# First batch's dilated values read from the load's own buffer, one tail-value load per batch, and a new table of scheduling biases

## The chip, the cores and the metric

One core of a Trainium2 chip runs the whole program. The metric is the device time of one execution in microseconds (us). The engines named here are PE (TensorE, matrix multiplication and transposes; PEld is its weight load), DVE (VectorE), ACT (ScalarE), POOL (GpSimd) and SP (SyncE, which here only issues DMAs). A DMA moves data between DRAM and the core's memory; SP and POOL each have a queue of them. "L901" is line 901 of the kernel before; behind L408 the changed file is one to eleven lines longer.

## What is computed

Two stages: attention with a sliding window over 8 batches of 8 heads, 576 positions and 64 channels, and a feed-forward layer over the 4608 rows that come out of it.

```python
scores = scale * np.matmul(q, k.transpose(0, 1, 3, 2))
rel = pos[:, None] - pos[None, :]
mask_plain = (rel >= 0) & (rel < window)                                  # window = 32
mask_dil = (rel >= 0) & (rel < window * dilation) & (rel % dilation == 0) # dilation = 4
masks = [mask_plain if h < H // 2 else mask_dil for h in range(H)]
attn = softmax(where(masks, scores, -1e9))
x = (attn @ v) reordered to (4608, 512)
h = x @ w_in                                   # 512 -> 2048
out = (h / (1 + exp(-beta * h))) @ w_out       # 2048 -> 512
```

Heads 0 to 3 are the plain ones, heads 4 to 7 the dilated ones. Inputs and output are float32; the matmuls run on bf16 copies.

## The kernel before

**Attention of a batch.** A dilated head is taken apart into its four residues (position modulo 4), each a sequence of 144, of which the first 128 are handled as one block and the last 16 as "the tail". In the list of steps of a batch, KD and QD are the transposes of dilated keys and queries (PE L483, blocks of 96), KP and QP those of the plain heads (L493, 64x64 quarters), S2, S3 and S0x, S1x the scores (L697 dilated; L725 or L761 plain), T the scores of the tail (L666), V the products of probabilities and values (L802 dilated, L818 plain), U the tail's (L787), X and Y the transposes of the result into xT, the layer's input with channels on the partitions (L855, L870, L840). For batches 0 and 1 all of these are done by PE; from batch 2 on (BY_DMA) the last step goes through DRAM with a DMA transpose issued by SP (L547), and from batch 3 on (DIRECT) keys and queries are cast by a DMA into DRAM (tiles s) and transposed by DMA on their way in (L474).

**Values.** A batch's values come in three kinds of load, all issued by POOL at L408 with a cast from float32 to bf16. The plain heads' go to vp. The dilated heads' first 128 rows go to vd16 (batches 0 to 2) or to a part of the tile st, and an instruction named spread (L257 in the helper copy) copies them into vd, whose rows have 80 entries: 64 values, and a column of ones at entry 64, so that one matmul with 65 columns gives the weighted sum and the sum of weights. The tail's go to vt, in two loads, one for each residue pair c.

**Layer.** For each of 9 blocks t of 512 rows, slot_h makes 16 slices fb of the hidden layer (four matmuls of 512 columns each, L901; the first four slices of t = 0 are split at column 288 as the first batch's columns come in parts), then tanh on ACT (L910) and the gate on DVE (L915). block_cols multiplies with w_out (L936) and copies the result out (L951, L953). w_in comes in three loads: slices 0 to 3, 4 to 7 and 8 to 15; w_out in two.

**What sets the order.** Nothing is issued in the order of the source. All work is recorded as operations with dependencies, a due time vt, a duration for every engine that may take it, and for DMAs a size, a rate and a latency. Plan.run then builds one order per engine by playing the engines' clocks with these figures: at each step it takes, among the operations that could start within NEAR of the earliest, the one with the lowest due time. NUDGE is a table that gives some operations, by their number, a bias in nanoseconds on their start. Where PE would stand idle before 80 us of planned time, a filler (L1057 or L1059, a matmul on zeros) is put in. The figures only shape the order; on the chip each instruction waits for semaphores. DMAs of POOL take eight semaphores in turn, so a load also waits until the eighth load before it has landed. An engine executes strictly in its order, and so does each DMA queue's issuing engine: what stands behind a waiting instruction waits with it.

**The start.** POOL issues the first loads (queries of dilated heads, keys and queries of plain heads, then vd16, vp) between small instructions that build an identity (ident_b, ident_f) and the masks (add_d, add_P, mask_t, mask_d, mask_n); the first keys come by SP. Then come w_in, the second batch's loads, w_out. From batch 3 on, a tiny POOL instruction named pace (L1015) waits for the columns of xT two batches earlier before that batch's loads are issued.

Of the kernel before, what the change touches and what calls it, by code (L numbers as in the profile page):

```python
# [10 lines left out]
ACT = mybir.ActivationFunctionType  # L11
# [29 lines left out]
class Plan:  # L41
# [3 lines left out]

    CAPS = {"h": 4, "p": 4, "o": 3, "z": 4, "a": 8, "s": 5, "w": 6}
    SWITCH = 95
    NUDGE = {6: 2500, 32: -2500, 44: 150, 45: -400, 58: -150, 72: 60, 76: -400, 88: -400, 96: 60,
        98: 150, 104: -2500, 105: 900, 107: 900, 161: 150, 167: 900, 172: 60, 173: 400, 199: -900,
        208: 150, 214: -400, 216: 2500, 221: 900, 223: 150, 234: -400, 238: -150, 239: 150,  # L50
        241: 150, 248: -60, 250: -2500, 257: -400, 259: -400, 264: 60, 275: 900, 277: 400,
        278: -2500, 279: 400, 292: -150, 311: 900, 318: -400, 323: 150, 326: -900, 329: 400,
        333: -400, 337: 60, 342: -900, 347: -400, 363: 2500, 364: -900, 365: -150, 367: -2500,
        372: 400, 379: 60, 380: -400, 383: -150, 390: 400, 392: -2500, 394: -400, 408: -150,
        415: -900, 425: -150, 494: -900, 500: -150, 519: 60, 526: 900, 528: -60, 529: 900,
        535: 900, 538: 2500, 553: 900, 589: -60, 597: -2500, 633: 2500, 661: -900, 663: 400,
        669: 2500, 671: 2500, 680: 400, 681: -400, 684: 150, 685: -150, 807: 400, 916: -60,
        943: 150, 948: 150, 1083: 2500}
    LAT = {"PE": 210, "ACT": 45, "DVE": 45, "POOL": 60, "SP": 0}
    NEAR = {"PE": 40, "ACT": 60, "DVE": 60, "POOL": 60, "SP": 0}  # L60

# [137 lines left out]
def kernel(  # L199
# [10 lines left out]
    nc = tc.nc  # L210
    P = 128
    B, H, S, D = q.shape
# [5 lines left out]
    WIN = 32  # L218
    C = 4
    CT = S // C  # L220
    UT = CT - P
    KTL = UT + WIN
# [11 lines left out]
    DIRECT = 3  # L234
# [14 lines left out]
    plan = Plan(range(8))  # L249
# [6 lines left out]
    def copy(e, out, in_):  # L256
# [25 lines left out]
    ptd = const([P, 2, 2, 4, P], BF16, "ptd")  # L282
# [8 lines left out]
    st = [const([P, 2 * RD * D + 2 * RP * D], BF16, f"st{i}") for i in range(2)]  # L291
    std = [s[0:2 * GD, 0:2 * RD * D].rearrange("p (x e) -> p x e", x=2) for s in st]
    stp = [s[:, 2 * RD * D:].rearrange("p (x e) -> p x e", x=2) for s in st]
    vd16 = const([P, 4, C, D], BF16, "vd16")
    vd16_of = [vd16[:]] * DIRECT + [st[b % 2][:, 0:1024].rearrange(
        "p (h T d) -> p h T d", h=4, T=C) for b in range(DIRECT, B)]
# [8 lines left out]
    vd = [const([P, 4, C, DV], BF16, f"vd{i}") for i in range(2)]  # L305
    vt_ = [const([2 * KTL, 2, 4, DV], BF16, f"vt{i}") for i in range(2)]
# [3 lines left out]
    mm = lambda n: n / 2.4 + 2.5  # L310
# [34 lines left out]
    fill3 = plan.op([("DVE", 500)], t_fill3, vt=-7.8)  # L345
# [5 lines left out]
    fill4 = plan.op([("POOL", 800)], t_fill4, vt=-1.2)  # L351
# [58 lines left out]
    def load(queue, args, deps, vt, kb, rate=.4, issue=750, lat=1100, late=0):  # L410
        return plan.op(
            [(queue, issue)],
            lambda e: dma(queue, *args), deps, vt, dma=kb * 1024 / rate / 1000, lat=lat, late=late)

    def direct_qk(b, z, h0, deps, vt):
        rows, n, dst = ((2 * GD, RD, std) if h0 else (P, RP, stp))
        src = bass.AP(tensor=(k, q)[z].tensor, offset=(k, q)[z][b, h0].offset,
                      ap=[[n * D, rows], [2 * S * D, 2], [1, n * D]])
        return load("POOL", (dst[z], src), deps, vt, 576, .41 if b or not (z and h0) else .29, lat=1100 if b else 1450)

    def first_keys():

# [22 lines left out]

    def direct_vd(b, deps, vt, tdeps=()):
        src = v[b, 4:8].rearrange("h (t T) d -> t h (T d)", T=C)[0:P]
        out = [load("POOL", (vd16_of[b].rearrange("p h T d -> p h (T d)"), src), deps, vt, 512, .39, lat=1450 if b < DIRECT else 4000, late=0 if b <= DIRECT else 4000)]
        for c in range(2):
            src = bass.AP(tensor=v.tensor, offset=v[b, 4].offset + ((P - WIN) * C + c) * D,  # L450
                          ap=[[2 * D, 2 * KTL], [S * D, 4], [1, D]])
            out.append(load("POOL", (vt_[b % 2][:, c, :, 0:D], src), list(tdeps), vt + (1.255 if b == 0 else .02 if b < DIRECT else 0) + .001 + .001 * c, 96, .3, lat=1100 if b < DIRECT else 4000, late=0 if b <= DIRECT else 4000))
        return out

    scratch = {}
# [47 lines left out]
    def war(*keys):  # L503
        return [o for key in keys for o in last.get(key, ())]

    def used(key, o):
        last.setdefault(key, []).append(o)

    def wrote(*keys):
        for key in keys:  # L510
            last[key] = []
# [39 lines left out]
    def attention(b, ld, names, vts):  # L551
# [3 lines left out]
        kv = b % 2  # L555
        if b < DIRECT:
            quarters = {}
            for n in [x for x in names if x[0] in "KQ"]:
                z, kind, i = "KQ".index(n[0]), n[1], int(n[2])
                vt = vt_of[n]  # L560
# [8 lines left out]
                elif kind == "D":  # L569
                    g = Group("a")  # L570
# [4 lines left out]
                if kind == "P":  # L575
                    g, tr = quarters[z][0][i], quarters[z][1]
# [16 lines left out]
        def mixed(e):  # L593
            copy(e, dkt[kv], dk[kv][:, :, :, CT - KTL:].rearrange("p r h k -> p h k r"))
        o = plan.op([("DVE", 450), ("POOL", 550), ("ACT", 500)], mixed,
                    (steps["KD0"] + steps["KD1"] if b < DIRECT else ready["D"][0:1]) + war(("dkt", kv)), vt_of["T"] - .01, sbuf=True)
# [4 lines left out]
        for c in range(2):  # L601
            def padded(e, c=c):
# [3 lines left out]
            o = plan.op([("DVE", 250), ("POOL", 500), ("ACT", 290)], padded,  # L606
                        (steps["QD0"] + steps["QD1"] if b < DIRECT else ready["D"][1:]) + [fill1] + war(("qt", kv)),
                        vt_of["T"] - .01, sbuf=True)
# [6 lines left out]
        vdeps = {}  # L615
        vt = vt_of["zVAL"]
        vdeps["P", 1] = [ld["vp"][-1], (fill3, fill4)[kv], fill3]
        vdeps["P", 0] = [ld["vp"][0], (fill3, fill4)[kv], fill3]
        def spread(e):
            copy(e, vd[kv][:, :, :, 0:D], vd16_of[b])  # L620
        o = plan.op([("POOL", 1100), ("DVE", 620), ("ACT", 1030)], spread,
                    [ld["vd"][0], (fill3, fill4)[kv]] + war(("vd", kv)), vt, sbuf=True)
        used("vd16" if b < DIRECT else ("st", kv), o)
        wrote(("vd", kv))
        vdeps["D"] = [o]
        vdeps["T"] = ld["vd"][1:] + [(fill3, fill4)[kv]]

        sdone, vdone, xback = {}, {}, []
# [29 lines left out]
        for name in [n for n in names if n[0] in "ST"]:  # L658
            vt = vt_of[name]
# [119 lines left out]
        for name in [n for n in names if n[0] in "VU"]:  # L779
# [17 lines left out]
            if x >= 2:  # L797
                def values(e, x=x, j=j, g=g):
                    pv = bank(g)[:, 0:4 * (D + 1)].rearrange("p (r h e) -> p r h e", r=2, h=2)
                    for r in range(2):  # L800
                        for a in range(2):
                            nc.tensor.matmul(pv[:, r, a], lhsT=ptd[:, x - 2, j, 2 * r + a],  # L802
                                             rhs=vd[kv][:, 2 * (x - 2) + a, 2 * r + j, 0:D + 1],
                                             start=True, stop=True)
                vop = plan.op([("PE", 4 * mm(D + 1))], values, [sdone[x, j]] + vdeps["D"], vt, acquire=g)
                used(("vd", kv), vop)
                used(("pt", x, j), vop)
                normed((x, j), vop, g, vt, P, 4,
                       lambda g=g: bank(g)[:, 0:4 * (D + 1)].rearrange("p (r h e) -> p r h e", r=2, h=2),
                       xdm[:].rearrange("p (r c) x h d -> p c r x h d", c=2)[:, j, :, x - 2], "xdm")  # L810
                continue
# [281 lines left out]
```

## Time and profile before

| what | value |
| --- | --- |
| median of 3 runs | 300.2 us (299.62 to 300.37) |
| the profiled execution, its own time | 299.95 us |
| its span in the profile | 298.3 us |
| mean granted clock of TensorE | 0.999 |
| L936, products with w_out | 136.6 us busy, 608 matmuls |
| L901, products with w_in | 134.8 us busy, 584 matmuls |
| fillers L1057 and L1059 | 108 and 39 matmuls, 3.0 and 5.8 us busy |
| L802, dilated values | 128 matmuls, 7.7 us busy |
| POOL's DMA queue | 60336 packets, 18.58 MB |
| tail-value loads | 16, of 48.0 KB each, median 10.0 us from issue to landing |

The profile is of one execution on the chip. The view of waits names an engine and line, what it waited for, and "us in total, times, longest us". The chain that ended last is followed back from the last instruction; its rows are start, length and what. A timeline row is start, length of the group, engine, line, operation, tiles, shape, count, and in brackets the idle time before it with what ended it. Matmuls are pipelined: the length of one in the profile (379 ns for 512 columns) is longer than the distance from one start to the next (216 ns), and it is the distance that counts for the time. "DMA to landing" is the time from the issue of a DMA to its last byte's arrival.

### The profile page before, as it was taken

The numbers are of one execution on the slowest core, as the hardware profiler recorded it, in microseconds if no ns is written. First come the engines' busy times: TensorE is split into PE (matmuls) and PEld (weight loads), VectorE is DVE, ScalarE is ACT, GpSimd is POOL, SyncE is SP. The second block draws the span as 40 slices with busy tenths as digits, with TensorE's granted clock in tenths as the row PEclk, the third lists the DMA queues.
The fourth block names the chain that finished last, engine by engine and source line by source line (L and its number), as shares of the span: only waits on it lengthen the run. The fifth ranks groups of instructions, "written<-read, shape, count | busy, mean of one in ns | idle before, by whom it ended". The sixth has DMA issues, their size and how long they took to land.

```text
span 298.3 us, 6224 instructions
## 1 busy us (share of the span) xinstructions
PE 293.0 (98%) x2424; PEld 149.8 (50%) x2424; DVE 186.1 (62%) x422; ACT 169.8 (57%) x308; POOL 90.4 (30%) x126
## 2 busy tenths in 40 slices
PE   8999999999999999999999999999999999999995
PEld 6765456545554445444544454445444444444454
DVE  4879668888767658774589358936891075433300
ACT  3768876867456738642487348634862376445311
POOL 8987354654283026600551065000100000000000
PEclk9999999999999999999999999999999999999999
DMA  7999999999979995999999989995115200010122
GB/s 150 187 208 202 206 196 210 154 163 184 185 124 226 151 199 124 171 136 240 184 188 155 200 174 196 162 186 147 38 31 124 73 0 36 35 37 37 63 76 73
DMA packets 111249, 42.00 MB, mean 141 GB/s; under 512 B 87620, under 2 KB 104596, under 8 KB 111220
## 3 DMA queue, kind: packets, MB, share of 16 engines
q0 software_dynamic: 60336, 18.58, 59.6%
q1 hardware_dynamic: 50740, 22.95, 36.4%
q8 instruction: 19, 0.31, 0.4%
q10 hardware_dynamic: 144, 0.07, 0.1%
q14 instruction: 10, 0.08, 0.1%
HBM read 37.76 MB, written 18.87 MB: 190 GB/s over the span
## 4 chain that ended last, share of the span: by engine, by line
PE 86%; DMA 8%; POOL 2%; DVE 1%; issue 1%; ACT 0%; POOLq 0%
PE bank L936 42%; PE bank L901 36%; DMA w_out_bf<-in_moe_w_out_dram 6%; DMA w_in_bf<-in_moe_w_in_dram 2%; PE bank L818 2%; PE bank L697 1%; PE bank L802 1%; PE bank L725 1%; POOL vp L408 1%; PE bank L787 1%; PE bank L666 0%; PE bank L761 0%; POOL st L408 0%; DVE g L915 0%; PE bank L493 0%
## 5 line engine op out<-in xcount | busy, mean ns | idle before, releaser
L936 PE MATMUL bank<-w_out_bf,g 128*128 128x512 bf16 (+2 forms) x608 | 136.6, 368 | 0.4 <-DMA w_out_bf<-in_moe_w_out_dram 0.4
L901 PE MATMUL bank<-xT,w_in_bf 128*128 128x512 bf16 (+2 forms) x584 | 134.8, 376 | 0.1
L915 DVE SCALAR_TENSOR_TENSOR g<-tnh,bank 128x512 bf16<-128x512 bf16 x144 | 96.5, 683 | 51.5 <-ACT tnh L910 50.3
L910 ACT ACTIVATE tnh<-bank,beta_half 128x512 bf16<-128x512 f32 x144 | 98.4, 690 | 53.2 <-PE bank L901 47.4
L901 PEld LDWEIGHTS <-w_in_bf 128*128 128x128 bf16 x584 | 55.1, 98 | 60.6 <-issue 0.2
L936 PEld LDWEIGHTS <-g 128*128 128x128 bf16 x608 | 55.2, 98 | 57.8 <-DMA w_out_bf<-in_moe_w_out_dram 0.5
L951 ACT ACTIVATE osb<-bank 128x512 f32<-128x512 f32 (+1 forms) x30 | 17.6, 592 | 34.1 <-PE bank L936 29.5
L633 ACT ACTIVATE ptd<-bank 128x512 bf16<-128x512 f32 x32 | 17.0, 600 | 21.4 <-PE bank L697 21.4
L633 ACT ACTIVATE pt<-bank 128x384 bf16<-128x384 f32 (+1 forms) x54 | 21.1, 463 | 6.5 <-PE bank L725 4.1
L637 DVE TENSOR_TENSOR pt<-pt,mask_n 128x384 bf16<-128x384 bf16 (+1 forms) x39 | 14.5, 378 | 12.1 <-ACT pt L633 11.6
L653 DVE TENSOR_TENSOR xsp<-bank,rcp 96x384 bf16<-96x384 f32 x32 | 17.7, 554 | 1.1
L637 DVE TENSOR_TENSOR ptd<-ptd,mask_d 128x512 bf16<-128x512 bf16 x25 | 10.9, 448 | 11.3 <-ACT ptd L633 10.4
L953 DVE TENSOR_SCALAR osb<-bank 128x512 f32<-128x512 f32 (+2 forms) x8 | 4.9, 607 | 20.5 <-PE bank L936 20.5
L652 DVE RECIPROCAL rcp<-bank 128x4 f32<-128x4 f32 (+2 forms) x72 | 12.8, 177 | 3.5 <-PE bank L818 1.4
L408 POOL DMA_DIRECT2D vt<-in_v_dram x16 | 13.7, 864 | 4.0 <-DMA w_out_bf<-in_moe_w_out_dram 2.9
L637 POOL TENSOR_TENSOR pt<-pt,mask_n 128x288 bf16<-128x288 bf16 (+1 forms) x7 | 5.3, 764 | 31.2 <-ACT pt L633 31.2
L653 DVE TENSOR_TENSOR xdm<-bank,rcp 128x256 bf16<-128x256 f32 x32 | 13.6, 424 | 1.1
L408 POOL DMA_DIRECT2D s<-in_k_dram x10 | 12.9, 1286 | 0.6 <-issue 0.6
L1015 POOL COPY pace<-xT 1x2 bf16<-1x2 bf16 x4 | 0.7, 176 | 39.2 <-DMA xT<-x 39.2
L408 POOL DMA_DIRECT2D s<-in_q_dram x10 | 12.2, 1220 | 0.1
L818 PEld LDWEIGHTS <-pt 128*128 128x128 bf16 x192 | 8.9, 97 | 4.4
L408 POOL DMA_DIRECT2D vp<-in_v_dram x9 | 10.2, 1129 | 1.0 <-DVE g L915 0.8
(113 smaller groups left out, 186.8 us busy)
## 6 DMA issues: line engine op xcount, KB each, us to landing
out_dram<-osb SPq DMA_DIRECT2D x35, 256.0 KB, 3.8
s<-in_q_dram POOLq DMA_DIRECT2D x10, 288.0 KB, 10.2
s<-in_k_dram POOLq DMA_DIRECT2D x10, 288.0 KB, 9.0
w_out_bf<-in_moe_w_out_dram POOLq DMA_DIRECT2D x2, 1024.0 KB, 17.4
vp<-in_v_dram POOLq DMA_DIRECT2D x7, 288.0 KB, 13.5
st<-in_q_dram POOLq DMA_DIRECT2D x6, 288.0 KB, 10.0
x<-xsp SPq DMA_DIRECT2D x12, 144.0 KB
st<-in_k_dram POOLq DMA_DIRECT2D x5, 288.0 KB, 13.2
```

The source lines that it names most:

```text
L408: {"POOL": nc.gpsimd, "SP": nc.sync}[queue].dma_start(out=out, in_=in_)
L633: nc.scalar.activation(out=w(), in_=sc(), func=ACT.Exp, scale=SCALE)
L637: E[e].tensor_tensor(out=w(), in0=w(), in1=m(), op=ALU.mult)
L652: nc.vector.reciprocal(out=r, in_=p[..., D])
L653: nc.vector.tensor_tensor(out=dst, in0=p[..., 0:D], in1=r.unsqueeze(len(p.shape) - 1).to_broadcast(list(p.shape[:-1]) + [D]), op=ALU.mult)
L818: nc.tensor.matmul(pv[:, a, h2, :], lhsT=lhs, rhs=vp[kv][:, (2 * x + h2) * NI + 3 * j + a, 0:D + 1], start=True, stop=True)
L901: nc.tensor.matmul(bank(g)[:, a:z], lhsT=w_in_bf[:, kt, fb * P:(fb + 1) * P], rhs=xT[:, kt, xo + a:xo + z], start=(i == 0 and kt == kts[0] ...
L910: nc.scalar.activation(out=th[:, 0:n], in_=bank(g)[:, 0:n], func=ACT.Tanh, scale=beta_half[:, fb:fb + 1])
L915: nc.vector.scalar_tensor_tensor(out=g_t[t % 2][:, fb, c0:c0 + n], in0=th[:, 0:n], scalar=1.0, in1=bank(g)[:, 0:n], op0=ALU.add, op1=ALU.mult)
L936: nc.tensor.matmul(bank(g)[:, lo:hi], lhsT=g_t[t % 2][:, fb, tb * P:(tb + 1) * P], rhs=w_out_bf[:, fb, lo:hi], start=(fb == 0), stop=(fb = ...
L951: nc.scalar.mul(out=ob[:, lo:hi], in_=bank(g)[:, lo:hi], mul=0.5)
L953: nc.vector.tensor_single_scalar(out=ob[:, lo:hi], in_=bank(g)[:, lo:hi], scalar=0.5, op=ALU.mult)
```

## The change

It has four parts.

1. For batch 0 spread is left out. The dilated values are read by the matmuls straight from vd16, 64 columns at a time, and the column of ones from vd by a second matmul of one column with the same weights. The 16 matmuls of 65 columns of that batch become 16 of 64 and 16 of 1. The buffer vd16 is now marked as read by these matmuls, not by the copy.
2. The two loads of tail values of each batch become one, with twice the bytes.
3. Three rates in the planner's model change: query and key loads of batch 2 (.41 to .36) and the load of batch 2's dilated values (.39 to .33). They have no effect but through the order.
4. NUDGE has 100 entries instead of 85, all different. The numbering of the operations has changed with parts 1 and 2, so the entries can't be compared one by one.

```diff
-    NUDGE = {6: 2500, 32: -2500, 44: 150, 45: -400, 58: -150, 72: 60, 76: -400, 88: -400, 96: 60,
...
+    NUDGE = {10: -150, 47: 2500, 60: -2500, 64: 60, 66: 150, 67: 60, 75: 400, 82: -2500, 86: 400,
...
-        return load("POOL", (dst[z], src), deps, vt, 576, .41 if b or not (z and h0) else .29, lat=1100 if b else 1450)
+        return load("POOL", (dst[z], src), deps, vt, 576, .36 if b > 1 else .41 if b or not (z and h0) else .29, lat=1100 if b else 1450)
...
-        out = [load("POOL", (vd16_of[b].rearrange("p h T d -> p h (T d)"), src), deps, vt, 512, .39, lat=1450 if b < DIRECT else 4000, late=0 if b <= DIRECT else 4000)]
-        for c in range(2):
-            src = bass.AP(tensor=v.tensor, offset=v[b, 4].offset + ((P - WIN) * C + c) * D,
-                          ap=[[2 * D, 2 * KTL], [S * D, 4], [1, D]])
-            out.append(load("POOL", (vt_[b % 2][:, c, :, 0:D], src), list(tdeps), vt + (1.255 if b == 0 else .02 if b < DIRECT else 0) + .001 + .001 * c, 96, .3, lat=1100 if b < DIRECT else 4000, late=0 if b <= DIRECT else 4000))
+        out = [load("POOL", (vd16_of[b].rearrange("p h T d -> p h (T d)"), src), deps, vt, 512, .33 if b == 2 else .39, lat=1450 if b < DIRECT else 4000, late=0 if b <= DIRECT else 4000)]
+        src = bass.AP(tensor=v.tensor, offset=v[b, 4].offset + (P - WIN) * C * D,
+                      ap=[[2 * D, 2 * KTL], [D, 2], [S * D, 4], [1, D]])
+        out.append(load("POOL", (vt_[b % 2][:, :, :, 0:D], src), list(tdeps),
+                        vt + (1.255 if b == 0 else .02 if b < DIRECT else 0) + .001, 192, .3,
+                        lat=1100 if b < DIRECT else 4000, late=0 if b <= DIRECT else 4000))
...
-        o = plan.op([("POOL", 1100), ("DVE", 620), ("ACT", 1030)], spread,
-                    [ld["vd"][0], (fill3, fill4)[kv]] + war(("vd", kv)), vt, sbuf=True)
...
+        if b:
+            o = plan.op([("POOL", 1100), ("DVE", 620), ("ACT", 1030)], spread,
+                        [ld["vd"][0], (fill3, fill4)[kv]] + war(("vd", kv)), vt, sbuf=True)
+            used("vd16" if b < DIRECT else ("st", kv), o)
+            wrote(("vd", kv))
+            vdeps["D"] = [o]
+        else:
+            vdeps["D"] = [ld["vd"][0], fill3]
...
-                            nc.tensor.matmul(pv[:, r, a], lhsT=ptd[:, x - 2, j, 2 * r + a],
-                                             rhs=vd[kv][:, 2 * (x - 2) + a, 2 * r + j, 0:D + 1],
+                            lhs, at = ptd[:, x - 2, j, 2 * r + a], (slice(0, P), 2 * (x - 2) + a, 2 * r + j)
+                            if b:
+                                nc.tensor.matmul(pv[:, r, a], lhsT=lhs, rhs=vd[kv][at][:, 0:D + 1], start=True, stop=True)
+                                continue
+                            nc.tensor.matmul(pv[:, r, a, 0:D], lhsT=lhs, rhs=vd16_of[b][at], start=True, stop=True)
+                            nc.tensor.matmul(pv[:, r, a, D:D + 1], lhsT=lhs, rhs=vd[kv][at][:, D:D + 1],
                                              start=True, stop=True)
-                vop = plan.op([("PE", 4 * mm(D + 1))], values, [sdone[x, j]] + vdeps["D"], vt, acquire=g)
+                vop = plan.op([("PE", 4 * mm(D + 1) + (0 if b else 100))], values, [sdone[x, j]] + vdeps["D"], vt, acquire=g)
                 used(("vd", kv), vop)
+                if b == 0:
+                    used("vd16", vop)
```

The orders that come out differ in these ways. On PE there are 16 more matmuls of one column and four fillers fewer. On POOL the first load of dilated queries comes ahead of ident_f instead of behind it; ident_f comes just ahead of the first w_in load; the two selects of mask_t come ahead of it too, in front of add_d, where they stood behind it. The query load between the first and the second w_in load is that of batch 1's dilated heads; that of its plain heads is issued behind the first w_out load. On PE batch 1's plain query transposes (36 of 64x64) stand behind slice 8 of t = 0 instead of ahead of L901's first matmul, and 12 transposes of its dilated queries ahead of it instead of behind. The number of DMAs on SP is the same.

## The prediction

> **What bounds the kernel now.** I read the page's first two parts, then the waits of PE, the chain that ended last, and the timelines of POOL and PE up to 40 us.
>
> ```profile
> PE 293.0 (98%) x2424; PEld 149.8 (50%) x2424; DVE 186.1 (62%) x422; ACT 169.8 (57%) x308; POOL 90.4 (30%) x126
> ...
> PEclk9999999999999999999999999999999999999999
> ```
>
> PE is busy for 293.0 of 298.3 us at the full granted clock, so only two things can change the time: the amount of work in PE's order, and its waits.
>
> ```profile
> PE bank L936 <- DMA w_out_bf<-in_moe_w_out_dram: 0.4, 1, 0.4
> PE bank L493 <- DMA st<-in_q_dram: 0.2, 1, 0.2
> PE bank L687 <- POOL add_d L359: 0.2, 1, 0.2
> ```
>
> The waits are small, and these lie before 35 us. (Busy ends are modelled; from start to start the first is 0.56 us: eight L787 matmuls from 34.01, 0.03 each, end their issue at 34.25, and L936 starts at 34.81. One more of 0.28 us stands at 186.0.) There is thus at most about 2 us to win. The chain tells what the early stretch hangs on:
>
> ```profile
> 3.02 1.40 POOL st L408 x2
> ...
> 6.32 1.76 POOL vp L408 x2
> ...
> 9.58 6.91 DMA w_in_bf<-in_moe_w_in_dram
> 16.50 0.28 issue
> 16.78 17.99 DMA w_out_bf<-in_moe_w_out_dram
> 34.77 0.04 issue
> 34.81 1.04 PE bank L936 x4
> ```
>
> POOL's own sequence of loads and small mask instructions leads to the first w_in load; from there POOL's DMA queue leads to PE. The queue lands in order of issue:
>
> ```profile
> 9.58 0.78 POOL L408 DMA_DIRECT2D w_in_bf<-in_moe_w_in_dram  x1
> 10.37 0.55 POOL L376 TENSOR_SCALAR_AFFINE_SELECT mask_t<-mask_t 128x256 bf16<-128x256 bf16 x1
> 10.99 0.52 POOL L379 TENSOR_SCALAR_AFFINE_SELECT mask_t<-mask_t 128x256 bf16<-128x256 bf16 x1
> 11.49 0.72 POOL L408 DMA_DIRECT2D st<-in_q_dram  x1
> 12.20 1.51 POOL L408 DMA_DIRECT2D w_in_bf<-in_moe_w_in_dram  x2
> ```
>
> and, from the view of the tile w_in_bf:
>
> ```profile
> DMA to landing us min/median/max: 6.9/8.3/12.5
> ```
>
> The three w_in loads land 6.9, 8.3 and 12.5 us after issues at 9.58, 12.20 and 12.95 (the second of the pair): at 16.5, 20.5 and 25.45. The first came 2.9 us behind the last vp load (7.20 + 6.4 = 13.6), though the third moved twice as much in 4.95. So it was already late by issue, by some 0.4 us: the queue ran dry.
>
> ```profile
> 18.44 1.04 PE L901 MATMUL bank<-xT,w_in_bf 128*128 128x512 bf16 x4
> ...
> 20.01 7.52 PE L901 MATMUL bank<-xT,w_in_bf 128*128 128x512 bf16 x42
> ```
>
> The 41st matmul of L901 is the first to read the third w_in load. Six stand before 20.01; from there come 2 of 512 columns (0.216 from start to start), 8 of 288 (0.123), 8 of 224 (0.096) and 16 of 512, so it starts at 20.01 + 0.43 + 0.98 + 0.77 + 3.46 = 25.65, with 0.2 us in hand. This point, "fb 8", is where I join the two orders.
>
> **The change, part by part.** *The copy removed.* The first batch's spread took 0.43 us on DVE at 12.03; the values waited for it (PE L802 at 12.57, the load landed at 5.33 + 6.4 = 11.7). Up to 0.8 us at the head of batch 0; PE reaches L901 sooner. By itself this only moves it into the wait for w_in.
>
> *Sixteen one-column matmuls added, all before fb 8.* No row shows one. Bounds: 0.013 us (36 transposes of 64x64 in 0.48) and 0.031 (a 65-column one); I take 0.025, 0.4 us in all, since with full-height weights it is nearer the second. Four fillers of 0.109 fewer give 0.44 back, two row-height switches fewer 0.19 (0.095 each, L901 to L697 starts 0.312 apart instead of 0.216). PE's whole order is 0.2 us shorter.
>
> The Trainium skill ("TensorE: Matmul & The Clock Gate", section "Wait — 56ns, not 53.3ns?") states a floor of about 25 ns from start to start however small N is, which speaks against splitting a matmul. The 64x64 transposes of this trace go below it, at 13 ns. By the rule the pieces cost 0.4 us, by that row 0.2.
>
> *One tail load instead of two.* The same bytes. Issue on POOL falls by one of 0.67 to 0.71 us a batch, none of it on a chain behind 16 us, where POOL waits for landings anyway (2.93 us at 35.05). In the queue the two landed 0.38 apart (14.32 + 12.9, 15.00 + 12.6), so 0 to 0.38 is saved; I take 0, as the bytes are equal.
>
> The skill's "DMA: Bandwidth & Descriptors", section "Anatomy of one DMA — SWDGE (gpsimd) path", puts a fixed 2.0 us on each DMA; by it each batch would save 2 us, by these rows at most 0.38.
>
> *The first batch's value buffer is freed by PE instead of DVE.* Batch 1's load into it issued at 21.04, behind the second w_in's landing (20.5, the eighth load before it); PE's reads (L802 at 12.57 and 13.71) end near 14. Nothing, unless they slip 7 us.
>
> *The new biases, in POOL's order.* The first query load now stands ahead of ident_f (0.38 us, 0.81 to 1.19), which moves to just ahead of the first w_in; and both selects of mask_t move ahead of it, from behind. From the first load to w_in was 8.0 us (1.58 to 9.58); it becomes 8.0 + 1.12 (10.37 to 11.49) + 0.38 = 9.5. Starting at 1.2 that is 10.7; at 0.81, if the 0.39 us of issue ahead of the first load is hidden, 10.3. With 6.9 to landing, w_in lands at 17.2 to 17.6, and the third, 8.95 behind it as now, at 26.1 to 26.6. Four loads stand in this stretch of the queue in both orders (three w_in and one 576 KB query load, now the other one). If the first w_in is not bound by issue, the low bound is the queue 0.38 earlier: 25.1. I take 26.4: **fb 8 starts at 26.45, 0.8 us late**. PE's work ahead of fb 8 is 0.7 us shorter than before (5 fillers 0.55, 36 quarter transposes 0.48 and 6 switches 0.57 go; 12 dilated transposes 0.51 and 0.4 come), so it would arrive about 25.0 unhindered, and waits.
>
> *PE behind fb 8.* The 36 quarter transposes of batch 1 come here (+0.48), 12 transposes leave (-0.51), one filler (+0.11) and four switches (+0.38) come: +0.46. The queue behind 26.4 by its own steps: keys 1.4, tail 0.7, w_out 5.8, keys 1.25 give 27.8, 28.5, 34.35 and 35.6. PE's order reaches their users at 28.2, 28.45, 34.25 and 35.2. So the w_out wait goes (-0.56), and two small ones come, tail values 0.15 and quarter transposes of batch 1 some 0.25: +0.4, between 0 (landings 0.4 earlier) and 0.9 (batch 1's tail mask, now on POOL, and batch 2's loads late too). The 0.28 at 186 I leave as it is.
>
> Sum: 0.8 + 0.46 - 0.56 + 0.4 = **+1.1 us**: span 299.4 and an execution of 299.95 + 1.1 = 301.05. The profiled one lies 0.25 below the runs' median; 300.2 + 1.1 = 301.3. I forecast 301.2.
>
> *Later loads.* In POOL's order the fifth batch's casts, with their pace instruction at 83.31, now stand behind one mask on the fourth batch's scores (ready near 88): 5.6 us later. SP has the fourth batch's column transposes (issued 98.70 and 102.25, 3.5 to landing: 105.75) behind that batch's key and query transposes. Their user, L901, is at 111.08 now, so 5.3 us of cover; 3 to 5 are used up. The fifth batch's query copies on ACT and DVE, with tanh and gate instructions queued behind them, may wait a microsecond or two; PE, with four banks of L901 results of 0.86 us each, waits for those only past 3. Cost 0, at most 1 if the casts also run slower.
>
> **The rivals.**
>
> *Not late after all.* The first w_in lands by the queue's pace and PE meets fb 8 at 25.65 as now: +0.46 - 0.56 + 0.4 = +0.3, 300.5. For it: the queue starts 0.38 earlier. Against: the dry 0.4 us ahead of w_in now, and 1.1 us more POOL work in front.
>
> *Faster.* The queue's earlier start carries through, the third w_in lands at 25.1 and PE is there: -0.55 + 0.46, and the waits at w_out and 186 both fall away (-0.84), none new: -0.9, 299.3. It decides from the first w_in landing at or before 16.2. For it: the copy's 0.8 us and fewer fillers. Against: w_in would have to land 5.5 us behind its issue, with 6.9 in the row.
>
> *The columns of the fourth batch late.* The casts slip 5.6 us and land 2 us slower besides, the column transposes land at 113.4 where PE is at 112.2: +1.1 + 1.2, 302.5. For it: POOL's and SP's fixed orders. Against: 5.3 us of cover, and before no wait stands there; that also says that nothing can be won at that place.
>
> **How the numbers follow.** Forecast 0.53, not late 0.22, faster 0.13, columns 0.12. Runs of this kernel lie within 0.75 us, so 0.3% (0.9 us) is about what can be told from no change: 299.3 to 301.1. The forecast lies on its edge; three fifths of it above gives 0.32, with the columns 0.44, some of "not late" 0.02: slower 0.46, same 0.41, faster 0.13. The forecast's own range is 300.3 to 302.0 (w_in 26.1 to 26.6, new waits 0 to 0.9). To hold eight in ten: 299.6, half the way into "faster", to 302.5.
>
> **What would show it.** First w_in issued past 10.2 and landed past 17; the third near 26.4 and PE's wait at the 41st L901 matmul naming w_in; no wait at the first L936; no wait of PE near 111. Wrong, if the third w_in lands before 25.6, or if any wait behind 60 us exceeds 0.5.

## The result and the profile after

| what | before | after |
| --- | --- | --- |
| median of the runs | 300.06 us (6 runs, 299.62 to 300.37) | 301.5 us (6 runs, 301.24 to 302.9) |
| ratio to before, 95% interval | | 1.0058 (1.0037 to 1.008) |
| profiled execution, span | 299.95 us, 298.3 us | 301.24 us, 299.5 us |
| start of PE's last matmul | 294.95 us | 296.24 us |

The change makes the kernel 0.58% slower; the profiled execution lost 1.29 us. Lines of the changed file are numbered differently: L901 is now L912, L936 L947, L493 L495, L787 L792, L633/L637 L638/L642, L653 L658, L1015 L1026. The experiments below have numbers of their own.

The page's first part, then the whole view of PE's waits, of the kernel after:

```profile
PE 294.5 (98%) x2436; PEld 149.9 (50%) x2436; DVE 184.2 (61%) x415; ACT 170.8 (57%) x310; POOL 87.2 (29%) x122
```

```profile
PE bank L1068 <- DVE warm L317: 1.1, 1, 1.1
PE bank L866 <- DVE xdm L658: 0.3, 1, 0.3
PE bank L912 <- DMA w_in_bf<-in_moe_w_in_dram: 0.2, 1, 0.2
PE bank L912 <- DMA xT<-x: 0.2, 1, 0.2
```

PE is as full as before. The wait for w_out is gone; in its place stand one for the third w_in load and one for the columns xT. (The first line, PE's wait for its first operand, stands in the view of before with the same 1.1 us. In the second, xdm is the dilated heads' result, which DVE divides by the sum of weights.) The timeline of POOL and the landing line of the tile w_in_bf show the queue:

```profile
1.40 0.86 POOL L409 DMA_DIRECT2D st<-in_q_dram  x1 [0.87 <-POOLq L1088]
...
4.26 0.56 POOL L377 TENSOR_SCALAR_AFFINE_SELECT mask_t<-mask_t 128x256 bf16<-128x256 bf16 x1
4.89 0.52 POOL L380 TENSOR_SCALAR_AFFINE_SELECT mask_t<-mask_t 128x256 bf16<-128x256 bf16 x1
...
10.91 0.78 POOL L409 DMA_DIRECT2D w_in_bf<-in_moe_w_in_dram  x1
11.69 0.64 POOL L409 DMA_DIRECT2D st<-in_q_dram  x1
12.32 1.52 POOL L409 DMA_DIRECT2D w_in_bf<-in_moe_w_in_dram  x2
```

```profile
DMA to landing us min/median/max: 5.7/8.3/13.1
```

The first w_in is issued 1.33 us later than before (10.91 against 9.58) and lands 0.1 us later (16.6 against 16.5); the third, issued at 13.09, lands at 26.24 instead of 25.43. A DMA lands in sixteen parts. The first parts of the three w_in loads come 1.0 us later than before (16.00, 19.99 and 24.99 against 14.97, 19.02 and 23.97), but the last part, for which PE waits, trailed by 1.53 us before and by 0.62 us now at the first load, by 1.46 and 1.25 us at the third. PE's timeline where it meets the third load, at the first product with w_out, and at the fourth batch's columns:

```profile
24.63 1.43 PE L912 MATMUL bank<-xT,w_in_bf 128*128 128x512 bf16 x7
26.29 1.90 PE L912 MATMUL bank<-xT,w_in_bf 128*128 128x512 bf16 x8 [0.23 <-DMA w_in_bf<-in_moe_w_in_dram]
...
33.33 1.04 PE L912 MATMUL bank<-xT,w_in_bf 128*128 128x512 bf16 x4
34.20 1.03 PE L947 MATMUL bank<-w_out_bf,g 128*128 128x512 bf16 x4
35.16 0.48 PE L495 MATMUL bank<-ident_b,st 64*64 64x64 bf16 x36
...
110.83 1.04 PE L947 MATMUL bank<-w_out_bf,g 128*128 128x512 bf16 x4
112.06 1.02 PE L912 MATMUL bank<-xT,w_in_bf 128*128 128x512 bf16 x4 [0.19 <-DMA xT<-x]
```

The seven matmuls from 24.63 would be followed by the next at 25.9 (the last starts at 25.80, its 224 columns take 0.1); it starts at 26.29, so PE waits 0.39 from start to start. Four matmuls of 512 columns take 0.86: L947 follows at 34.20 without a gap. At 110.83 + 0.86 = 111.70 PE could go on, and starts at 112.06: 0.36 us for the columns. Two more waits from start to start are 0.20 at 43.1 (L792, the second batch's tail) and 0.27 at 183.3, the heir of the 0.28 at 186.0. The chain that ended last names what the columns hang on:

```profile
13.09 13.15 DMA w_in_bf<-in_moe_w_in_dram
26.29 1.90 PE bank L912 x8
...
88.90 6.29 DMA s<-in_q_dram
95.25 3.98 SPq L476
99.40 3.16 SPq L549
102.61 9.31 DMA xT<-x
112.06 1.02 PE bank L912 x4
```

The casts of the fifth batch are issued at 88.3 and 88.9, where they were at 83.55 and 84.15; SP's transposes follow, and the second column transpose needs 9.31 us to land.

Where the time went, from starts of matmuls ("41st" is fb 8; the waits are those above):

| | before | after | difference |
| --- | --- | --- | --- |
| start of the 41st product with w_in | 25.64 | 26.29 | +0.65 |
| from there to the last matmul | 269.31 | 269.96 | +0.65 |
| waits in that stretch | 0.56 + 0.28 | 0.20 + 0.36 + 0.27 | -0.01 |
| the stretch without its waits | 268.47 | 269.13 | +0.66 |

So PE is 0.65 late at the 41st product: 0.25 because it comes there later itself (25.90 against 25.64) and 0.39 in the wait for the third w_in load. More work behind it costs another 0.66, and the wait won at w_out is given back at 43 and 112.

### The profile page after: what moved, and what is told of

Same layout as the page of the kernel before. It is cut to its first block, busy times and chain, and to the rows that moved or that the text cites. A ratio compares the mean times of both kernels' runs of the same rounds, so it can differ in the third digit from the quotient of the medians.

```text
span 299.5 us, 6234 instructions
## 1 busy us (share of the span) xinstructions
PE 294.5 (98%) x2436; PEld 149.9 (50%) x2436; DVE 184.2 (61%) x415; ACT 170.8 (57%) x310; POOL 87.2 (29%) x122
## 3 DMA queue, kind: packets, MB, share of 16 engines
q1 hardware_dynamic: 50740, 22.95, 36.6%
## 4 chain that ended last, share of the span: by engine, by line
PE 81%; DMA 10%; issue 3%; SPq 2%; POOL 1%; DVE 1%; ACT 0%; POOLq 0%; ACTq 0%
PE bank L947 36%; PE bank L912 34%; DMA w_in_bf<-in_moe_w_in_dram 4%; DMA xT<-x 3%; DMA s<-in_q_dram 2%; PE bank L829 1%; SPq L476 1%; PE bank L1070 1%; PE bank L702 1%; SPq L549 1%; PE bank L1068 1%; PE bank L809 1%; PE bank L485 1%; PE bank L495 1%; PE bank L730 1%
## 5 line engine op out<-in xcount | busy, mean ns | idle before, releaser
L947 PE MATMUL bank<-w_out_bf,g 128*128 128x512 bf16 (+2 forms) x608 | 137.2, 368 | 0.0
L912 PE MATMUL bank<-xT,w_in_bf 128*128 128x512 bf16 (+2 forms) x584 | 135.9, 376 | 0.5 <-DMA w_in_bf<-in_moe_w_in_dram 0.2
L912 PEld LDWEIGHTS <-w_in_bf 128*128 128x128 bf16 x584 | 54.8, 98 | 61.0 <-issue 1.0
L947 PEld LDWEIGHTS <-g 128*128 128x128 bf16 x608 | 55.1, 98 | 57.4
L962 ACT ACTIVATE osb<-bank 128x512 f32<-128x512 f32 (+1 forms) x33 | 19.5, 591 | 37.3 <-PE bank L947 34.0
L638 ACT ACTIVATE pt<-bank 128x384 bf16<-128x384 f32 (+1 forms) x54 | 21.1, 462 | 7.8 <-PE bank L730 5.8
L638 ACT ACTIVATE ptd<-bank 128x512 bf16<-128x512 f32 x32 | 16.7, 604 | 14.5 <-PE bank L702 14.5
L642 DVE TENSOR_TENSOR ptd<-ptd,mask_d 128x512 bf16<-128x512 bf16 x27 | 12.1, 447 | 14.3 <-ACT ptd L638 13.3
L642 DVE TENSOR_TENSOR pt<-pt,mask_n 128x384 bf16<-128x384 bf16 (+1 forms) x36 | 13.2, 374 | 11.7 <-ACT pt L638 11.2
L658 DVE TENSOR_TENSOR xsp<-bank,rcp 96x384 bf16<-96x384 f32 x32 | 17.7, 554 | 1.1
L642 POOL TENSOR_TENSOR pt<-pt,mask_n 128x288 bf16<-128x288 bf16 (+1 forms) x10 | 7.6, 773 | 32.1 <-ACT pt L638 32.0
L658 DVE TENSOR_TENSOR xdm<-bank,rcp 128x256 bf16<-128x256 f32 x32 | 13.6, 424 | 1.1
L964 DVE TENSOR_SCALAR osb<-bank 128x512 f32<-128x512 f32 (+2 forms) x5 | 2.8, 555 | 16.6 <-PE bank L947 16.6
L409 POOL DMA_DIRECT2D vp<-in_v_dram x9 | 11.6, 1295 | 0.5 <-DMA st<-in_k_dram 0.5
L1026 POOL COPY pace<-xT 1x2 bf16<-1x2 bf16 x4 | 0.8, 188 | 33.6 <-DMA xT<-x 33.6
L829 PE MATMUL bank<-vp,pt 128*128 128x65 bf16 x192 | 9.6, 193 | 0.0
## 6 DMA issues: line engine op xcount, KB each, us to landing
st<-in_q_dram POOLq DMA_DIRECT2D x6, 288.0 KB, 10.3
```

Source lines behind the costliest of these rows:

```text
L409: {"POOL": nc.gpsimd, "SP": nc.sync}[queue].dma_start(out=out, in_=in_)
L638: nc.scalar.activation(out=w(), in_=sc(), func=ACT.Exp, scale=SCALE)
L642: E[e].tensor_tensor(out=w(), in0=w(), in1=m(), op=ALU.mult)
L658: nc.vector.tensor_tensor(out=dst, in0=p[..., 0:D], in1=r.unsqueeze(len(p.shape) - 1).to_broadcast(list(p.shape[:-1]) + [D]), op=ALU.mult)
L829: nc.tensor.matmul(pv[:, a, h2, :], lhsT=lhs, rhs=vp[kv][:, (2 * x + h2) * NI + 3 * j + a, 0:D + 1], start=True, stop=True)
L912: nc.tensor.matmul(bank(g)[:, a:z], lhsT=w_in_bf[:, kt, fb * P:(fb + 1) * P], rhs=xT[:, kt, xo + a:xo + z], start=(i == 0 and kt == kts[0] ...
```

## The experiments

Each kernel was timed beside before on the same chip. All but w_cut and after_again hold this scaffold: the orders that Plan.run builds are kept in a list (engine, operation) and issued from it, so that one entry can be moved and all others stay.

```diff
-            o.fn(e)
+            self.todo.append((e, o))
...
     plan.run(filler, 80000.0)
+    # one edit of plan.todo
+    plan.emit()
```

| kernel | median us | ratio to before (95%) |
| --- | --- | --- |
| part1 | 299.98 | 0.9994 (0.9984 to 1.0003) |
| parts12 | 299.87 | 0.9989 (0.9979 to 0.9999) |
| before_fwd | 301.0 | 1.0032 (1.0018 to 1.0046) |
| after_again | 301.96 | 1.0059 (1.0044 to 1.0074) |
| maskt_back | 301.55 | 1.0065 (1.0035 to 1.0095) |
| mask_dve | 301.22 | 1.0035 (1.0023 to 1.0047) |
| both_back | 301.14 | 1.0031 (1.0017 to 1.0045) |
| pace_fwd | 301.6 | 1.0046 (1.0029 to 1.0063) |
| xsp_fwd | 301.89 | 1.0059 (1.0044 to 1.0074) |
| w_cut | 302.07 | 1.0065 (1.0052 to 1.0078) |
| xsp_cut | 302.03 | 1.0061 (1.0045 to 1.0077) |
| mask_dve2 | 300.86 | 1.0021 (1.0009 to 1.0033) |

**The parts without the new order: parts12 and part1.** part1 is before with the diff's part 1 alone. parts12 adds part 2: the single load is issued in the place of the pair's first.

```diff
+    for pair in twins.values():
+        plan.todo.pop(max(plan.at(o) for o in pair))
```

> The kernel before with parts 1 and 2 of the change alone (values used where they land, one tail load a batch), every other instruction in the order of before. Theory (the loss comes from the new biases' order, not from these parts): the copy's wait at the head of batch 0 goes, 16 one-column matmuls add 0.2 to 0.4 us ahead of the 41st product with w_in, where PE has 0.2 in hand: 300.1 to 300.5 against 300.1 for before, that matmul starting at 25.5 to 25.9. The wait at the first product with w_out shrinks by the tail load's shorter time in the queue, 0.56 to 0.2 to 0.56. Rival (the parts themselves cost what the change loses, by the one-column matmuls' distance or the single load's landing): 301.0 or more, with PE waits named after vd or vt.

> The kernel before with part 1 alone (first batch's dilated values used where they land). Theory: within 0.3 us of before, 300.0 to 300.4; PE reaches the first product with w_in up to 0.8 us sooner or waits for w_in's landing instead, and the 41st starts at 25.5 to 25.9. The distance from one 64-column matmul to the next 64-column one of the same line, with the one-column one between, is 0.04 to 0.06 us. Rival: the column matmuls cost more, 300.8 or above.

parts12 is the fastest kernel of this study, faster than before by 0.1% with an interval that just ends below 1; part1 can't be told from before. PE's waits in parts12, the whole view, and its timeline where the one-column matmuls stand:

```profile
PE bank L1079 <- DVE warm L329: 1.1, 1, 1.1
```

```profile
13.57 0.19 PE L824 MATMUL bank<-vd,ptd 128*128 128x64 bf16 x1
13.60 0.17 PE L825 MATMUL bank<-vd,ptd 128*128 128x1 bf16 x1
...
34.73 0.41 PE L805 MATMUL bank<-vt,ptt 96*128 96x65 bf16 x8
34.97 1.03 PE L958 MATMUL bank<-w_out_bf,g 128*128 128x512 bf16 x4
```

Eight pairs take 13.57 to 14.01: 0.055 us a pair, 0.024 more than one matmul of 65 columns (0.031). No other wait is named. The 41st product starts at 26.36, 0.72 later than before, and yet the last matmul starts 0.12 sooner (294.83): the two waits of before, 0.84 together, took up the lateness. So in before's order a 41st product up to 0.84 late is nearly free, and the loss of the change lies in the new order, which parts 3 and 4 make together; no run tells these two apart. The rival falls.

**The selects of mask_t: before_fwd and maskt_back.**

```diff
+    plan.move(mask_tail, ahead=adds["D"])        # before_fwd: before, selects as after
...
+    plan.move(mask_tail, behind=w_in_ld[0])      # maskt_back: after, selects as before
```

> The kernel before with one thing done: on POOL the two selects of mask_t stand ahead of add_d, where the change has put them. Theory: the first w_in is issued 1.1 us later (10.7 instead of 9.58), the third lands at 26.2 instead of 25.45, and w_out, 9.3 behind it in the queue, at 35.5 instead of 34.77; PE waits for both, 0.8 us more in all: 300.9. Rival (w_in is bound by the queue's pace): third w_in at 25.5, time unchanged, 300.1.

> The changed kernel with one thing undone: on POOL the two selects of mask_t stand behind the first w_in load again, as before the change. Theory (w_in is late by issue): the first w_in is issued 1.1 us earlier, at 9.8 instead of 10.91, the third lands at 25.4 instead of 26.24, PE starts the 41st matmul of L912 without a wait at 25.9 instead of 26.29, and all behind it moves with it: 0.4 us less than the changed kernel, 301.1. Rival (the third w_in is slow in itself, 5.65 us behind the second instead of 4.95, because of the loads beside it; the first landed only 0.1 later than before): it still lands at 26.2, and the time stays at 301.5.

In before the selects' new place costs 0.9 us, in after taking it back wins nothing that can be told. PE's waits in before_fwd say why the first is dearer than the w_in queue alone:

```profile
PE bank L506 <- DMA st<-in_q_dram: 1.4, 1, 1.4
PE bank L1070 <- DVE warm L329: 1.1, 1, 1.1
PE bank L700 <- POOL add_d L372: 0.6, 1, 0.6
```

PE waits for add_d, which now stands behind the selects, so a staging buffer comes free later and POOL itself waits 1.2 us before it can issue a query load; the 41st product starts at 28.00, 2.36 late, of which before's two waits give back 0.84. The number 300.9 came out, by a mechanism half other than the one expected. In maskt_back w_in was issued at 9.75, and the first of its sixteen parts landed at 15.11 (after: 16.00), but the last at 17.43, and the third load at 26.47. The queue's fast parts follow the issue, the slowest part doesn't: the expectation missed.

**The third w_in load: w_cut.**

```diff
-    (w_in_bf[:, :, c0:c1], moe_w_in[:, c0:c1] ...
+    d0, d1 = ((0, 512), (512, 1152), (1152, 2048))[n]
+    (w_in_bf[:, :, d0:d1], moe_w_in[:, d0:d1] ...
```

> The changed kernel with the second and third w_in load cut at slice 9 instead of 8 (640 and 896 columns), so that the 41st product reads the second load. Theory (the wait there is for the third load's last byte; PE would be there at 25.9): no wait, that matmul at 25.9 to 26.0 instead of 26.29 to 26.66, and fb 9 at 26.8 just behind the landing. At the end 0 to 0.4 us less, since the wait near 112 takes back what the columns do not move with it: 301.1 to 301.6. Rival (the start at 26.3 was PE's own): no change at that matmul.

A miss that says something. PE's timeline in w_cut:

```profile
20.22 2.15 PE L912 MATMUL bank<-xT,w_in_bf 128*128 128x512 bf16 x16
22.95 5.32 PE L912 MATMUL bank<-xT,w_in_bf 128*128 128x512 bf16 x25 [0.58 <-DMA w_in_bf<-in_moe_w_in_dram]
```

The trace of w_cut holds 38 matmuls fewer than after's, two of them ahead of the 41st product. Set beside after's order, slice 4's first matmul is missing just ahead of 22.95: it started near 22.74, behind the larger second load's landing at 22.68, where PE could have gone on at 22.21, a wait of some 0.53 us. The 41st product is then the one at 26.38. It no longer waits, but it starts 0.09 us later than in after: the wait has moved to slice 4. In both cuts tried, PE meets the queue's bytes somewhere.

**The columns, first attempts: mask_dve, both_back, pace_fwd, xsp_fwd, xsp_cut.** mask_dve gives the mask that stands ahead of pace on POOL back to DVE; both_back is mask_dve and maskt_back together; pace_fwd leaves that mask on POOL, but issues pace and the first two of the loads behind it ahead of it; xsp_fwd exchanges two neighbours on DVE; xsp_cut is xsp_fwd and w_cut.

```diff
+    plan.todo[n] = ("DVE", plan.todo[n][1])                    # mask_dve: n is the mask
...
+    for o in early:                                            # pace_fwd: pace and two casts
+        plan.move(o, ahead=mask5)
...
+    plan.move(plan.todo[out4][1], behind=plan.todo[last][1])   # xsp_fwd: osb behind the last xsp
```

> The changed kernel with one mask (L642, 128x384, fourth batch's plain scores) on DVE instead of POOL, so that POOL's pace instruction of the fifth batch no longer stands behind it. Theory (the columns of the fourth batch were late through POOL's order): pace starts near 84 instead of 88.17, the fifth batch's casts and SP's transposes come 3 to 4 us earlier, the second column transpose lands near 108 instead of 111.9, PE has no wait at the first L912 near 112: 0.35 to 0.4 us less, 301.1, and the spread of the runs (301.24 to 302.9) shrinks below 0.8. Rival: the wait only moves (to the fifth batch's scores, or to DVE's gates behind the added mask of 0.5 us), or the spread has another cause: time and spread as in the changed kernel.

> Both of these together in the changed kernel. Theory: the two losses lie one behind the other on PE and add: 0.75 us less than the changed kernel, 300.75, still 0.6 over the kernel before: the work that the new order has put behind the 41st matmul and the w_out wait that it saves are left. Rival (the first gain is eaten by the next landing of the queue, as all of it until 57 us comes just in time): no more than 0.4 less, 301.1.

> The changed kernel with the fifth batch's pace instruction and its first two casts put ahead of the mask that delayed them on POOL, the mask staying on POOL right behind. Theory (the 0.36 us wait near 112 comes from the casts' being 5 us late, and with it the column transposes): pace at 85.4, casts at 85.6 and 86.2, no wait at the first matmul near 112, no new one near 88 to 90, and 0.3 to 0.4 us less than the changed kernel: 301.1 to 301.2. Rival (the column transposes are late by SP's order behind the key and query transposes, whatever the casts do, or the gain is lost later): 301.5, wait still there or another behind it.

> The changed kernel with two neighbours on DVE exchanged near 91 us: the last division of the fourth batch's plain heads (xsp) ahead of an output copy (osb) of 0.69 us. Theory (the fourth batch's columns are late because their result reaches SP 1.0 us later, behind that copy; the earlier casts of pace_fwd changed nothing): the second write of xsp issues at 91.2 to 91.3 instead of 91.9, the last column transpose lands 0.3 to 0.7 us sooner, at 111.2 to 111.6, and the wait near 112 goes: 301.1 to 301.3 where the changed kernel has 301.5 to 301.9. Rival (the four transposes run at the pace of the shared DMA engines, which the loads of POOL fill until 111 to 112, whenever SP starts): the landing stays at 111.9 to 112.4 and so does the time.

> Both edits, xsp_fwd and w_cut, in the changed kernel. Theory: both waits go, 0.7 to 0.9 us less than the changed kernel: 300.7 to 301.0; what is left against before (300.1) is the 0.49 us of PE work moved behind the 41st product and 0.2 us at the second batch's tail. Rival (the columns stay where they are): 301.5, the wait near 112 grown to 0.7 or more.

mask_dve has no wait at 112, but a new one of 0.44 us from start to start, since DVE reaches the mask behind a pair of divisions. PE's timeline in mask_dve:

```profile
88.22 1.02 PE L962 MATMUL bank<-w_out_bf,g 128*128 128x512 bf16 x4
89.52 0.54 PE L844 MATMUL bank<-vp,pt 128*128 128x65 bf16 x12 [0.28 <-DVE pt L656]
```

With PE later by that much, the missing wait proves little; its eight runs lie within 0.86 us. both_back has the same 0.44 and another 0.42 at 16.3 us (xdm again), no wait at 112, and with 301.14 misses its 300.75. pace_fwd refuted my first reading, that the first casts' lateness delays the columns. POOL's and PE's timelines in pace_fwd:

```profile
85.20 0.63 POOL L423 DMA_DIRECT2D s<-in_k_dram  x1
85.82 0.56 POOL L423 DMA_DIRECT2D s<-in_q_dram  x1
87.29 0.91 POOL L656 TENSOR_TENSOR pt<-pt,mask_n 128x384 bf16<-128x384 bf16 x1 [0.91 <-ACT pt L652]
88.15 0.84 POOL L423 DMA_DIRECT2D st<-in_v_dram  x1
...
92.03 2.27 POOL L423 DMA_DIRECT2D s<-in_k_dram  x1
```

```profile
110.80 1.04 PE L962 MATMUL bank<-w_out_bf,g 128*128 128x512 bf16 x4
112.16 1.02 PE L927 MATMUL bank<-xT,w_in_bf 128*128 128x512 bf16 x4 [0.32 <-DMA xT<-x]
```

The two casts are 3 us sooner, and the wait is still there (0.48). My second reading, SP's late start, fell with xsp_fwd: its columns landed at 112.68, no sooner, with a wait of 1.02. xsp_cut missed likewise (1.55 at 112).

**The columns, last attempt: mask_dve2.** The mask on DVE again, in the gap ahead of the tail's division. There it comes ahead of the exponential of its group, so one of the six groups of the fourth batch's plain scores goes unmasked. The same instructions run, but PE no longer waits for an exponential and then the mask in that group, which may help at 88.9.

```diff
+    plan.todo[n] = ("DVE", mask5)
+    plan.move(mask5, ahead=first)
```

> The changed kernel with the mask that stood ahead of the fifth batch's loads on POOL done by DVE again, this time in the gap ahead of the tail's division near 87.2 us instead of behind a pair of divisions, where it made PE wait 0.44 us at 88.9. Theory (the fourth batch's columns are late because all of POOL's loads behind that mask run 3 to 5 us later and then share the DMA engines with SP's transposes): pace at 85 to 86, all eight loads behind it at once, the last column transpose lands no more than 0.2 us later against PE's own position than before, so no wait near 112, and none near 88.9: PE's lag behind the kernel before stays at 0.9 to 1.3 us from 90 to 180 us, 301.0 to 301.3. Rival (the landing does not depend on those loads): a wait near 112 of 0.4 to 1.5 us as in the six executions with the loads late, 301.5 to 302.

PE's timeline in mask_dve2:

```profile
111.03 1.04 PE L964 MATMUL bank<-w_out_bf,g 128*128 128x512 bf16 x4
111.90 1.03 PE L929 MATMUL bank<-xT,w_in_bf 128*128 128x512 bf16 x4
```

No wait at 112 and none at 88.9, and 300.86 us. Its interval (1.0009 to 1.0033) lies below that of after_again. The 0.27 near 184 is gone as well; with the 0.56 at 112 that makes the 0.83 us by which PE gets from the 41st product to the end sooner than in after_again (269.24 against 270.07). The columns of all fourteen profiles, ordered by the issue of the last of the loads behind pace ("could go on" is PE's start without its wait):

| kernel | first cast issued | last cast issued | columns landed | PE could go on | wait |
| --- | --- | --- | --- | --- | --- |
| parts12 | 82.98 | 87.93 | 110.36 | 111.06 | 0 |
| before | 83.55 | 88.39 | 110.52 | 110.91 | 0 |
| part1 | 84.95 | 89.81 | 110.70 | 111.07 | 0 |
| before_fwd | 85.57 | 90.43 | 112.28 | 112.70 | 0 |
| both_back | 85.68 | 90.66 | 111.04 | 112.22 | 0 |
| mask_dve | 85.95 | 90.92 | 111.94 | 112.14 | 0 |
| mask_dve2 | 86.02 | 90.99 | 111.37 | 111.90 | 0 |
| pace_fwd | 85.20 | 92.03 | 112.02 | 111.68 | 0.48 |
| after | 88.29 | 93.25 | 111.92 | 111.70 | 0.36 |
| xsp_fwd | 88.38 | 93.35 | 112.68 | 111.79 | 1.02 |
| maskt_back | 88.42 | 93.40 | 112.08 | 111.83 | 0.38 |
| xsp_cut | 88.50 | 93.48 | 113.33 | 111.92 | 1.55 |
| after_again | 88.57 | 93.55 | 112.41 | 111.99 | 0.56 |
| w_cut | 88.62 | 93.60 | 113.06 | 112.03 | 1.16 |

The last column goes with the third, not with the second: last cast up to 91.0, no wait; from 92.0 on, always one. That the whole row of loads decides it, and not its first two, is less sure than this looks. In mask_dve the columns landed no sooner than in after (111.94 against 111.92), and PE only came later; and mask_dve2's landing lies 0.55 and 1.04 us ahead of the two profiles of the changed kernel, which themselves lie 0.49 apart.

That the column transposes are slower beside POOL's loads is in the traces. Each profile has twelve column transposes. By the last of its sixteen parts, each of the ten that run while POOL's queue moves next to nothing lands 3.1 to 5.5 us after its issue, in all fourteen profiles; the two of the fourth batch, which run beside the fifth batch's loads, take 8.2 to 10.2 us in every one, and the second lands 0.2 to 1.4 us behind the last cast. The DMA queues in before (packets, MB, and the time of their packets as a share of the sixteen engines'; q0 is POOL's, q1 SP's) while the second of these two was under way, 102.25 to 110.52, and then while another was, 139.59 to 143.32:

```profile
q1 hardware_dynamic: 3174, 1.01, 80.6%
q0 software_dynamic: 3328, 0.42, 78.1%
```

```profile
q1 hardware_dynamic: 3109, 0.93, 115.8%
```

The Trainium skill ("DMA: Bandwidth & Descriptors", section "Queues, rings and completion order") says that each engine takes turns between the queues that have work for it, which would do this. No run took the loads away to see the fourth batch's transposes alone.

**after_again** gave a second profile of the changed kernel.

> The changed kernel once more, for a second profile and as the yardstick of the others: 301.5 (301.2 to 302.0). Theory: PE's arrival at the 41st product with w_in at 25.9, started 26.0 to 26.6 as the last of the sixteen landings of the third w_in load falls; wait near 112 of 0.3 to 0.4 us again. Rival: the start at 26.29 was one execution's accident, and here it lies at 25.9 or before, at the same total.

The 41st product started at 26.66, after a wait of 0.93 for the third load, so the wait is no accident and PE's own arrival lies at 25.7 to 25.9; the waits at 43, 112 and 184 are 0.21, 0.56 and 0.27.

## Why the prediction was right, and where not

**Sum and forecast.** +1.1 was forecast, +1.29 measured between the profiles; 301.2 against a median of 301.5. The terms held worse than their sum, so the closeness is in part luck. Two of the signs given beforehand failed: the first w_in landed at 16.6, not past 17, and PE waits near 111, 0.36 in after and 0.56 in after_again, where 0.5 was to count against the prediction.

**fb 8, +0.8: it measured +0.65, with its legs wrong.** w_in was issued at 10.91, later than the 10.3 to 10.7 given. The 6.9 us from issue to landing, carried over as a constant, became 5.7; the first load landed at 16.6, not at 17.2 to 17.6. The third load's 26.1 to 26.6 held (26.24 and 26.62) by luck: it landed 9.6 and 10.1 us behind the first, not 8.95, which made up for the first's being early. And PE's unhindered arrival of 25.0 was 25.9: the step "PE's work ahead of fb 8 is 0.7 us shorter" counted work and no waits, but in after PE waits 0.44 us at 14.8 for xdm. That is half of the 0.9; the other half stays open. The late clock (below) is not it: in mask_dve2, where full clock came 2.5 us sooner, the arrival without the wait is 25.84. What makes the third load late in the new order stays open: in maskt_back, with w_in issued 1.16 sooner, it landed no sooner.

**PE behind fb 8, +0.46: measured +0.66** (0.55 to 0.66 over after, after_again and mask_dve2). Transposes and switches moved from a stretch where PE waits for w_in anyway to one where it has no slack. This is the half of the loss that no removed wait pays for, and the mechanism was right.

**w_out, -0.56: right**, and with more in hand than thought: w_out landed at 33.37, not 34.35, 0.8 ahead of its use.

**New small waits, +0.4: measured 0.20**, and at neither of the two places named; it stands at the second batch's tail.

**The 0.28 at 186, left as it is: right** for after (0.27).

**The columns, cost 0: the step that failed.** "3.5 to landing: 105.75 ... so 5.3 us of cover" took the landing from the view of the tile, which knows it for three of the twelve transposes (issued at 139.6, 170.3 and 222.8); all three ran while POOL's queue moved nothing. In before's own trace the last part of this one landed at 110.52, 8.3 us after its issue, and PE came at 110.91: a cover of 0.4 us. The trace had that number, and I used a median of others in its place. The rival "columns" priced the wait at 1.2 and gave it 0.12; it came at 0.36 and 0.56 in the two profiles of this kernel. The casts' slip, 5 us, was read rightly.

**One-column matmuls, 0.4 us: right**, 16 of 0.024. The estimate from the Trainium skill's floor ("TensorE: Matmul & The Clock Gate", section "Wait — 56ns, not 53.3ns?"), 0.4, agrees. The 64x64 transposes' 13 ns were no guide: in before's trace their starts come in fours, 3 or 4 ns apart, with mostly 21 or 22 ns from one four to the next.

**The copy's 0.8 us at the head: misread.** In before the copy ended at 12.46 and PE started L802 at 12.57 without a gap, so PE did not wait for it and there was nothing to win in that order. In part1 PE reaches L901 0.72 later than before (below); the end tells that parts 1 and 2 cost nothing.

**Tail load, 0: right.** part1 and parts12 lie 0.11 us apart, inside their intervals.

**The rivals.** "Not late" nearly held at the first w_in, which landed 0.1 later than before, and fell at the third, 0.81 later. "Faster" fell at the first, which had to land by 16.2. That parts 1 and 2 might win something by themselves was no rival of mine; the fastest kernel here, by 0.1%, has them alone in the old order.

## What to carry to other kernels

Take the landing of a DMA from that DMA's own parts, beside the start of its user, and not from the median of its kind, which may have run beside less traffic: cover is a difference of two moments. Where PE is full behind a gate and waits ahead of it, work moved from ahead of the gate to behind it costs its whole length, and lateness at the gate may cost nothing when the next wait takes it up. When a table of biases is made anew together with an edit, run the edit in the old order first.

## What was not expected of the hardware

**PE's clock rises at a moment of its own.** The first matmul starts at 1.13 or 1.14 us in every profile; by the trace's records full clock is granted from 3.96 us on in before, 6.44 in part1, 6.95 in parts12, 3.99 to 6.49 in the ten others that record it. Nine fillers of 256 columns in before, and the same nine in part1, from PE's timelines:

```profile
4.09 1.16 PE L1059 MATMUL bank<-zero 128*128 128x256 bf16 x9
```

```profile
4.15 2.10 PE L1077 MATMUL bank<-zero 128*128 128x256 bf16 x9
```

They start 0.21 us apart in part1 and 0.11 in before. How far this reaches depends on the order. In part1 PE is 0.75 us later than before at 9.8 us, and POOL, which waits for PE's transposes behind that, issues batch 1's query load 0.53 later (12.02 against 11.49):

```profile
12.02 0.72 POOL L421 DMA_DIRECT2D st<-in_q_dram  x1 [0.74 <-PE bank L506]
```

PE's wait for that load ends at 18.75 instead of 18.03, and L901 follows. The waits at w_out and at 186 then take this up. In the changed order PE is 0.63 later in after than in mask_dve2 (full clock from 6.49 and 3.99) at 7.0 us, but only 0.04 at 15.2, as mask_dve2 has waits in between. The Trainium skill ("TensorE: Matmul & The Clock Gate", section "What's actually happening") explains such a shift by a window that runs freely and does not start with the kernel, and states a spread of half a microsecond either way; here it was 3.0 us from first to last.

**The last of a load's sixteen parts.** For the first w_in load it trailed the first part by 0.53 us (mask_dve) to 3.41 us (before_fwd), and by 1.53 and 0.62 in before and after. A delay of issue under 1.5 us can vanish in that, as it did here, or not.
